# A convolution's backward pass: the input gradient's first three chunks with both outer leaves made from differences, the second gelu backward in channel halves, and a new order

## The chip, the cores and the metric

The kernel runs on one core of a Trainium2 chip. The metric is the device time of one execution in microseconds (us). In the listings PE is TensorE (PEld its weight loads), DVE is VectorE, ACT is ScalarE, POOL is GpSimd, and SP is the engine that issues most DMAs. "Weight load" and "matmul" are instructions; L1136 is line 1136 of the kernel.

## What is computed

A strided convolution along time (31 taps, stride 2, 256 channels in and out, two samples of 16000 steps, 7985 outputs), a group norm over time per channel, and a gelu; the outputs are the forward result and the gradients of x, w, gamma and beta.

```python
def _fwd_reference(x, w, gn_gamma, gn_beta):
    s = 2
    L = (T - K) // s + 1
    h = jnp.einsum('blc,cd->bld', x[:, 0:s * L:s, :], w[0])
    for i in range(1, K):
        h = h + jnp.einsum('blc,cd->bld', x[:, i:i + s * L:s, :], w[i])
    mu = jnp.einsum('bld->bd', h)[:, None, :] / L
    var = jnp.einsum('bld->bd', (h - mu) ** 2)[:, None, :] / L
    h = (h - mu) / jnp.sqrt(var + 1e-5)
    h = h * gn_gamma[None, None, :] + gn_beta[None, None, :]
    return _gelu(h)

def reference(x, w, gn_gamma, gn_beta, grad_out):
    _out, _vjp = jax.vjp(_f, x, w, gn_gamma, gn_beta)
    _grads = _vjp(grad_out)
    return (_out0, *[jnp.asarray(_g) for _g in _grads])
```

## The kernel before

**Stages.** The forward convolution of both samples (helpers named `f_`, matmuls at L506) runs first, with sample 0's gelu and gelu backward beside its second half. Then comes the input gradient (`input_grad`, matmuls at L1136): sample b = 0, chunks c = 0 to 3, then sample 1, chunks 0 to 3. The text numbers these t = 4b + c, 0 to 7. Last is the weight gradient (matmuls at L1351). Sample 1's gelu backward (`gelu_short`, eight units called by `gelu_batch`) runs beside the input gradient of sample 0; chunk 4 cannot begin before it has ended, since sample 1's gradient before the norm needs sums over the whole sample. Those sums are accumulated by ACT at L943, put together on DVE by `elem_finalize` (from the reduction at L978 on), and used by `e_load` and `e_comp` (L1015, L1017, L1033), which make the tile `ET` that a chunk starts from.

**A fast convolution of two levels.** The taps are split in a way that replaces four products of halves by three, first over branches (`br`: A, B, C), then over leaves (`lf`: A, B, C). A chunk is two halves (`pr`, 128 rows each) times three branches, so six units. A unit works in two PSUM tiles of 1024 fp32 columns. `g_three_b` and `g_three_ac` make the middle leaf B; its value is the seed for both outer leaves. Then the unit's outer leaves are made in the next unit's time, by the call `last(A)` and `last(C_)`:

- where (b, c, br) is in `GOC` ("both"), a third level of the same trick is used for the outer leaves as well. `g_outer` (4 matmuls) makes a product shared by two outputs, once with leaf C and once with leaf A. ACT copies it (`g_copy` into PSUM, `g_delta` into the tile `GSD`, L1165), DVE makes the seed with a subtraction (`g_seed`, L1199), and each outer leaf then takes 8 matmuls in `g_three_ac`, with differences that `third_two` makes on DVE. Such a unit has 36 matmuls. The results are evacuated by ACT (`keep`, L585), and DVE adds the middle branch for both leaves in one instruction of 2048 columns (L1213);
- elsewhere the seed is one copy by ACT (L585 inside PSUM), each outer leaf takes 16 matmuls in `g_leaf`, and DVE evacuates each of the two with the addition in it (L1217). Such a unit has 44 matmuls.

Before, branch B is always of the first kind, A and C from chunk 3 on. The weight sums that the first kind needs for A and C (`w2_outer`) are made after chunk 2.

**Gelu backward of sample 1.** One unit is one (c, e), 2048 columns, both channel halves (`dh`) side by side. ACT makes y and z from h (L916), DVE works on z (L920, L923), ACT makes two sigmoids (L926), DVE goes on (L920, L923), SP stores the result, ACT sums (L943, already by half). The tiles h and s come in rings of two, y and z in rings of one, grad_out in a ring of one.

**Staging.** After each chunk's first half `dl_turn` writes nine planes to DRAM for the weight gradient: for each, SP issues two transposes into a staging tile of the ring `DNO` (L319), and POOL two stores to `dld` (L314). The ring has four tiles. Since a plane (`GL`, `GS`, `ET`) is overwritten in the next chunk, its transposes must be over by then.

**Order.** Each engine works in program order, and its own queue of waits holds all that is behind. The program order is a table of operation numbers, `SEQUENCE`, made beforehand; `Plan.emit` issues operations in its order. Tiles have fixed addresses in one `arena`.

Of the kernel before, what the change touches and what calls it, by code (L numbers as in the profile page):

```python
# [1693 lines left out]
```

## Time and profile before

| | |
|---|---|
| runs | 1113.3, 1113.68, 1115.04 us |
| median | 1113.68 us |
| span of the profiled execution | 1111.2 us |

The span reaches from the first to the last instruction; what an execution takes beyond it lies around the program. The profiled execution's own time is not listed apart from its span; the median of the runs lies 2.5 us above that span. A group's row gives its line, engine, operation, shapes and count, then busy time in us and the mean of one in ns, then the engine's idle time just before it and what ended that.

### The profile page before, as it was taken

Reading aid. Unit: us, or ns where it says so; the run is one execution under the profiler, and the core shown is the slowest. Engines: PE = TensorE matmul, PEld = TensorE weight load, DVE = VectorE, ACT = ScalarE, POOL = GpSimd, SP = SyncE. Lnnn points to the kernel's source line nnn. Section 1 sums busy time; section 2 is a strip of 40 time slices with the busy share of each in tenths; the row PEclk is TensorE's granted clock in tenths of the full one; section 3 lists DMA queues with packets and bytes.
Section 4 is the critical chain, followed back from the end, with each engine's and each line's share of the span. In section 5 each row is a group of like instructions: output and inputs, shape, how many; then the busy total and the mean of one; then the engine's idle time right before and its main releaser. Section 6 shows DMA issues by size and latency. Waiting matters only on the chain.

```text
span 1111.2 us, 18967 instructions
## 1 busy us (share of the span) xinstructions
PE 1086.2 (98%) x7623; PEld 749.8 (67%) x7672; DVE 919.9 (83%) x900; ACT 578.9 (52%) x880; POOL 129.3 (12%) x233
## 2 busy tenths in 40 slices
PE   6999999999999989999999999999999999999998
PEld 4888899878787974444444444444587776678885
DVE  7987877889999999989897565644789699699995
ACT  1234434587988569899964566545413322111221
POOL 0000000000001003232332432251200000000000
PEclk9999999999999999999999999999999999999999
DMA  9979899876969789999999898577994959978888
GB/s 231 198 188 249 233 275 267 219 167 162 209 166 219 240 328 270 274 252 265 217 225 237 179 203 183 157 201 197 278 293 137 270 156 298 303 254 279 282 253 207
DMA packets 348806, 256.16 MB, mean 231 GB/s; under 512 B 234327, under 2 KB 315869, under 8 KB 343517
## 3 DMA queue, kind: packets, MB, share of 16 engines
q1 hardware_dynamic: 341613, 236.05, 81.8%
q0 software_dynamic: 7104, 18.89, 6.3%
q8 instruction: 60, 0.98, 0.4%
q14 instruction: 29, 0.24, 0.1%
HBM read 114.62 MB, written 84.45 MB: 179 GB/s over the span
## 4 chain that ended last, share of the span: by engine, by line
PE 89%; DVE 5%; issue 2%; DMA 1%; SPq 1%; ACT 1%; DVEq 0%
PE ps L1136 34%; PE ps L506 34%; PE ps L1351 21%; SPq L314 1%; DMA out_dram<-arena 1%; DVE arena L1437 1%; DVE ps L1461 1%; DMA arena<-in_w_dram 1%; DVE arena L1421 1%; DVE arena L1380 1%; DVE arena L1525 0%; DVE arena L581 0%; DVE arena L1417 0%; DVE arena L448 0%; DVE arena L1316 0%
## 5 line engine op out<-in xcount | busy, mean ns | idle before, releaser
L506 PE MATMUL ps<-arena 128*128 128x256 bf16 (+4 forms) x3464 | 396.6, 278 | 11.2 <-DMA arena<-in_x_dram 4.7
L1136 PE MATMUL ps<-arena 128*128 128x512 bf16 (+1 forms) x1787 | 388.1, 376 | 5.7 <-ACT ps L1165 3.6
L506 PEld LDWEIGHTS <-arena 128*128 128x128 bf16 x3464 | 338.2, 98 | 69.4 <-DMA arena<-in_x_dram 5.8
L1136 PEld LDWEIGHTS <-arena 128*128 128x128 bf16 x1824 | 178.5, 98 | 215.1 <-issue 2.9
L1351 PE MATMUL ps<-arena 128*128 128x256 bf16 (+1 forms) x2372 | 301.6, 289 | 3.4 <-DVE arena L1520 1.8
L1351 PEld LDWEIGHTS <-arena 128*128 128x128 bf16 x2384 | 233.2, 98 | 71.9 <-issue 2.3
L585 ACT ACTIVATE arena<-ps 128x1024 bf16<-128x1024 f32 (+1 forms) x121 | 122.1, 1022 | 213.0 <-PE ps L1351 77.3
L464 DVE TENSOR_TENSOR arena<-arena 128x2064 bf16<-128x2064 bf16 (+7 forms) x131 | 162.7, 1265 | 24.2 <-PE ps L506 23.0
L314 POOL DMA_DIRECT2D dld<-arena x144 | 104.6, 728 | 246.7 <-DMA arena<-arena 229.4
L1199 DVE TENSOR_TENSOR ps<-ps,arena 128x1024 f32<-128x1024 f32 x36 | 44.3, 1232 | 64.2 <-PE ps L1136 53.2
L1082 DVE TENSOR_TENSOR arena<-arena 128x1032 bf16<-128x1032 bf16 (+1 forms) x114 | 89.5, 813 | 9.5 <-POOL arena L1049 4.3
L551 ACT ACTIVATE ps<-ps 128x256 f32<-128x256 f32 x89 | 36.7, 412 | 85.6 <-PE ps L506 84.5
L1316 DVE TENSOR_TENSOR arena<-arena 128x4096 bf16<-128x4096 bf16 x30 | 68.3, 2287 | 0.5 <-DMA arena<-in_x_dram 0.3
L1165 ACT COPY ps<-ps 128x512 f32<-128x512 f32 x84 | 48.1, 575 | 33.7 <-PE ps L1136 30.0
L323 POOL MEMSET arena<- 128x104 bf16 (+11 forms) x52 | 12.0, 249 | 414.8 <-DVE arena L464 157.6
L923 DVE TENSOR_TENSOR arena<-arena 128x2048 bf16<-128x2048 bf16 (+1 forms) x48 | 57.5, 1197 | 3.0 <-ACT arena L926 1.3
L605 ACT ACTIVATE arena<-ps 128x512 bf16<-128x512 f32 (+1 forms) x64 | 37.0, 582 | 32.7 <-PE ps L506 28.2
L885 DVE TENSOR_TENSOR arena<-arena 128x2048 bf16<-128x2048 bf16 (+1 forms) x40 | 47.7, 1197 | 4.0 <-ACT arena L879 1.7
L1437 DVE TENSOR_TENSOR arena<-arena 128x2048 bf16<-128x2048 bf16 x40 | 48.5, 1220 | 2.4 <-PE ps L1351 2.4
L1461 DVE TENSOR_TENSOR ps<-ps,arena 128x1024 f32<-128x1024 f32 x24 | 29.1, 1227 | 19.5 <-PE ps L1351 19.5
L1453 ACT COPY ps<-ps 128x256 f32<-128x256 f32 x54 | 19.0, 360 | 47.8 <-PE ps L1351 46.7
L1525 DVE TENSOR_TENSOR arena<-arena 128x4608 bf16<-128x4608 bf16 x16 | 40.6, 2554 | 0.0
(92 smaller groups left out, 752.3 us busy)
## 6 DMA issues: line engine op xcount, KB each, us to landing
arena<-in_x_dram SPq DMA_DIRECT2D x36, 1024.0 KB
arena<-hd SPq DMA_DIRECT2D x40, 512.0 KB
dld<-arena POOLq DMA_DIRECT2D x144, 128.0 KB, 4.4
out_dram<-arena SPq DMA_DIRECT2D x14, 1024.0 KB
arena<-dld SPq DMA_DIRECT2D x18, 640.0 KB
arena<-dld SPq DMA_DIRECT2D x18, 576.0 KB
vl<-arena SPq DMA_DIRECT2D x36, 256.0 KB
arena<-vl SPq DMA_DIRECT2D x9, 1024.0 KB
```

The costliest lines, as they stand in the source:

```text
L314: lambda: e.dma_start(out=out, in_=in_), dma=np_ * ns / 16e3 * 1.03, ns=ns, tp=SH[pk], slack=slack)
L464: lambda: nc.vector.tensor_tensor(out=o, in0=a, in1=b, op=ALU.add))
L506: yield nc.tensor.matmul(ps[:, dh, cs], lhsT=wt, rhs=mv, start=s0, stop=False, skip_group_check=True)
L585: lambda: nc.scalar.activation(out=out, in_=ps, func=ACT.Copy, scale=scale))
L885: add("DVE", dve(nf), [o], [a, b_], lambda: V.tensor_tensor(out=o, in0=a, in1=b_, op=op))
L923: add("DVE", dve(nf), [o], [a, b_], lambda: V.tensor_tensor(out=o, in0=a, in1=b_, op=op))
L1082: lambda: nc.vector.tensor_tensor(out=o, in0=a, in1=b, op=ALU.subtract))
L1136: yield nc.tensor.matmul(ps[:, e, 0:wide], lhsT=lt, rhs=mv, start=s0, stop=False, skip_group_check=True)
L1165: add("ACT", act(512), [o], [i], lambda: nc.scalar.copy(out=o, in_=i))
L1316: add("DVE", dve(4096), [o], [a, b], lambda: nc.vector.tensor_tensor(out=o, in0=a, in1=b, op=ALU.add))
L1351: yield nc.tensor.matmul(ps[:, s, c0:c1], lhsT=lt, rhs=mv, start=s0, stop=False, skip_group_check=True)
L1437: add("DVE", dve(2048), [o], [u, v], lambda o=o, u=u, v=v: nc.vector.tensor_tensor(out=o, in0=u, in1=v, op=ALU.subtract))
```

## The change

- `GOC` now holds all branches of all chunks: in chunks 0 to 2, branches A and C become units of the first kind, 36 matmuls instead of 44. All weight sums of `w2_outer` are made ahead of the input gradient.
- `gelu_short` works on one channel half at a time: 16 half units instead of 8 units, with tiles of half the size in rings of the same counts; each half has its own load of h, its own store, and its own chain over ACT and DVE.
- Addresses move. The staging ring `DNO` has two tiles in chunks 0 to 3 (four before in chunks 0 to 2, four in chunk 3) and five after them. One of the two lies where the second `GSD` tile lies, so sample 0 uses one `GSD`, sample 1 two. `HO` (the input gradient's output tile) is one tile in all of sample 0, two in sample 1.
- `SEQUENCE` is new throughout, the forward and the weight gradient included. The matmuls of these two stages are the same in number.

```diff
@@ SEQUENCE
-7 10 4 1 11 8 5 9 2 13 3 6 12 20 14 15 36 30 38 39 29 35 32 40 33 31 24 34 37 23 41 42 50 48 47 45 21 51 44 49 46 43 22 53 59 54 26 52 64 28 60 83 84
...
+3511 3516 3503 3513 3517 3504 3505 3514 3518 3515
...
@@ tiles
-    HO = [sb(119232, 2, 4, 512), sb(GREG + 16704, 2, 4, 512)]
+    HO = [sb(119232, 2, 4, 512), sb(GREG + 20544, 2, 4, 512)]
...
-    DNO = {True: [sb(GREG + 28928 + 2048 * i, 2, 2, D) for i in range(4)], False: [sb(GREG + o, 2, 2, D) for o in (0, 2048, 25088, 27136)]}
+    DNO = {True: [sb(o, 2, 2, D) for o in (208960, 113088)], False: [sb(o, 2, 2, D) for o in (208960, *(GREG + 28736 + 2048 * i for i in range(4)))]}
...
@@ gelu_batch
-        tiles = [ring_of(k, 2, 4, HM) for k in rings]
+        tiles = [ring_of(k, *((2, 4, HM) if b == 0 else (4, HM))) for k in rings]
...
+                    for dh in range(2):
+                        gelu_short(b, c, e, dh, [r[(2 * n + dh) % len(r)] for r in tiles], go[:, dh])
...
@@ gelu_short
-    def gelu_short(b, c, e, tiles, go, oo):
+    def gelu_short(b, c, e, dh, tiles, go):
...
-        load(full[0].rearrange("p d k f -> p d (k f)"), hv, 524288, 2048, "ACT")
+        load(full[0].rearrange("p k f -> p (k f)"), hv, 262144, 2048, "ACT")
...
-        nf = 8 * wd
+        nf = 4 * wd
...
@@ dl_turn
-                ds = DNO[4 * b + c < 3]
+                ds = DNO[4 * b + c < 4]
...
-    gsc = [0]
+    gsc, bnow = [0], [0]
 
     def g_delta(pt):
-        gsc[0] += 1
-        g_copy(GSD[gsc[0] % 2], pt[:, 0])
+        gsc[0] = 1 - gsc[0] if bnow[0] else 0
+        g_copy(GSD[gsc[0]], pt[:, 0])
...
-        ho = HO[pr if both else 0]
+        ho = HO[pr if b else 0]
...
-    GOC = {(b, c, br) for b in range(NB) for c in range(NCK) for br in ORDER if 4 * b + c >= 3 or br == B_}
+    GOC = {(b, c, br) for b in range(NB) for c in range(NCK) for br in ORDER if (b, c, br) not in ()}
...
@@ the calls
-        if br == B_:
-            for lf in (C_, A):
-                w2_outer(lf, (B_,))
+        for lf in (C_, A):
+            w2_outer(lf, (MIR[br],))
...
-        if (b, c, pr, br) == (0, 2, 1, A):
-            for lf in (C_, A):
-                w2_outer(lf, (A, C_))
```

The first place is ACT in the middle of chunks 0 to 2. L943 is a sum of gelu, L916 its first two functions, L926 its sigmoids; L1165 is a copy of a shared product, L585 a seed (ps<-ps) or an evacuation (arena<-ps). Before:

```order
L943 ACTIVATE arena,esum_113<-arena 128x1024 x6
L1165 COPY ps<-ps 128x512
L916 ACTIVATE arena<-arena,stats 128x1024 x4
L585 ACTIVATE ps<-ps 128x1024
L585 ACTIVATE arena<-ps 128x1024
L926 ACTIVATE arena<-arena 128x2048 x2
L1165 COPY ps<-ps 128x512
L585 ACTIVATE arena<-ps 128x1024
```

The same engine in the changed kernel, where these lines are L951, L925, L935, L1173 and L591:

```order
L1173 COPY ps<-ps 128x512
L925 ACTIVATE arena<-arena,stats 128x1024
L591 ACTIVATE arena<-ps 128x2x512
L1173 COPY ps<-ps 128x512 x2
L1173 COPY arena<-ps 128x512
L951 ACTIVATE arena,esum_113<-arena 128x1024
L925 ACTIVATE arena<-arena,stats 128x1024
L951 ACTIVATE arena,esum_113<-arena 128x1024
L1173 COPY ps<-ps 128x512
L935 ACTIVATE arena<-arena 128x1024 x2
L591 ACTIVATE arena<-ps 128x2x512
```

Runs of one kind are gone: each half unit's few rows alternate with copies and evacuations of the convolution, of which there are more, and no row copies a seed any more.

The second place is DVE at the end of sample 1's gelu backward: the reduction of its sums (L978) and what follows to the scaling of chunk 4's tile (L1017, L1015, L1033). L1217 and L1199 belong to units of chunks 2 and 3, L452 and L1234 are weight sums. Before:

```order
L978 TENSOR_REDUCE small<-esum_113 128x4
L1082 TENSOR_TENSOR arena<-arena 128x2x516
L1217 TENSOR_TENSOR arena<-ps,arena 128x2x512
L980 TENSOR_TENSOR small<-stats,small 128x2
L1199 TENSOR_TENSOR ps<-ps,arena 128x1024
L1234 TENSOR_TENSOR arena<-arena 128x2048
L981 TENSOR_TENSOR small<-small 128x2
L452 TENSOR_TENSOR arena<-arena 128x2048
L982 TENSOR_TENSOR small<-stats 128x2
L983 TENSOR_TENSOR small<-stats,small 128x2
```

In the changed kernel (L932 the last gelu operations, L986 the reduction, L1023 and L1041 the scaling and the spreading into chunk 4's tile):

```order
L932 TENSOR_TENSOR arena<-arena 128x4x232 x3
L986 TENSOR_REDUCE small<-esum_113 128x4
L988 TENSOR_TENSOR small<-stats,small 128x2
L989 TENSOR_TENSOR small<-small 128x2
L990 TENSOR_TENSOR small<-stats 128x2
L991 TENSOR_TENSOR small<-stats,small 128x2
L992 SCALAR_TENSOR_TENSOR stats<-small 128x2
L993 SCALAR_TENSOR_TENSOR small<-small,stats 128x2
L994 TENSOR_TENSOR small<-stats 128x2
L995 SCALAR_TENSOR_TENSOR stats<-small 128x2
L1023 TENSOR_SCALAR arena<-arena,stats 128x2048
L1041 TENSOR_TENSOR arena<-arena 128x2x3x256
```

Work of the convolution that stood between these rows has moved ahead of them: on PE, 220 matmuls followed the reduction up to chunk 4's first before, and 44 do now.

More of the change, by code (lines that the diff above doesn't have):

```diff
@@ L350, in conv_stem_kernel @@
     GS = sb(190336, 2, 2, 2, 2, EM)
-    GL = {B_: sb(198656, 2, 2, 2, EM), A: sb(202816, 2, 2, 2, EM), C_: sb(102656, 2, 2, 2, EM)}
-    GU = {B_: sb(206976, 2, 2, EM), A: sb(106816, 2, 2, EM), C_: sb(108928, 2, 2, EM)}
+    GL = {B_: sb(198592, 2, 2, 2, EM), A: sb(202720, 2, 2, 2, EM), C_: sb(102656, 2, 2, 2, EM)}
+    GU = {B_: sb(206848, 2, 2, EM), A: sb(106816, 2, 2, EM), C_: sb(108928, 2, 2, EM)}
     GREG = 127424
-    HO = [sb(119232, 2, 4, 512), sb(GREG + 16704, 2, 4, 512)]
+    HO = [sb(119232, 2, 4, 512), sb(GREG + 20544, 2, 4, 512)]
     GSB = sb(115136, 2, 2, 512)
     GSD = [sb(o, 512, dt=FP32) for o in (111040, 113088)]
-    W2DO = {B_: sb(173696, 2, 2, 512), C_: sb(GREG + 29184, 2, 2, 512), A: sb(GREG + 33280, 2, 2, 512)}
-    GU2 = {br: sb(o, 2, 2, 2, 260) for br, o in zip(ORDER, (94336, 94336 + 4160, GREG + 12288))}
-    W2DC = {B_: sb(177792, 2, 2, 512), C_: sb(GREG + 4096, 2, 2, 512), A: sb(GREG + 8192, 2, 2, 512)}
-    DNO = {True: [sb(GREG + 28928 + 2048 * i, 2, 2, D) for i in range(4)], False: [sb(GREG + o, 2, 2, D) for o in (0, 2048, 25088, 27136)]}
-    assert GREG + 37952 <= REG
-    DG, DGT = sb(209664, P), sb(209920, P)
+    W2DO = {B_: sb(173696, 2, 2, 512), C_: sb(GREG, 2, 2, 512), A: sb(GREG + 4096, 2, 2, 512)}
+    W2DC = {B_: sb(177792, 2, 2, 512), C_: sb(GREG + 8192, 2, 2, 512), A: sb(GREG + 12288, 2, 2, 512)}
+    GU2 = {br: sb(o, 2, 2, 2, 260) for br, o in zip(ORDER, (94336, 94336 + 4160, GREG + 16384))}
+    DNO = {True: [sb(o, 2, 2, D) for o in (208960, 113088)], False: [sb(o, 2, 2, D) for o in (208960, *(GREG + 28736 + 2048 * i for i in range(4)))]}
+    assert GREG + 37184 <= 164608
+    DG, DGT = sb(164608, P), sb(164864, P)
     ident = DGT
@@ L850, in gelu_batch @@
                 oo = oos[n % len(oos)]
-                (gelu_unit if b == 0 else gelu_short)(b, c, e, [r[n % len(r)] for r in tiles],
-                                                      gt.rearrange("p k d f -> p d k f")[:, :, :, off:off + HM], oo)
+                go = gt.rearrange("p k d f -> p d k f")[:, :, :, off:off + HM]
+                if b == 0:
+                    gelu_unit(b, c, e, [r[n % len(r)] for r in tiles], go, oo)
+                else:
+                    for dh in range(2):
+                        gelu_short(b, c, e, dh, [r[(2 * n + dh) % len(r)] for r in tiles], go[:, dh])
                 n += 1
@@ L908, in gelu_short @@
         full = tiles
-        h, y, s, z, go = (t[:, :, :, 0:wd] for t in (*tiles, go))
-        hv, dv = (d[b][c][:].rearrange("p (d e f) -> p d e f", d=2, e=2)[:, :, e] for d in (h_d, dy_d))
-        load(full[0].rearrange("p d k f -> p d (k f)"), hv, 524288, 2048, "ACT")
-        for dh in range(2):
-            for o, k, fn in ((y, 7, ACT.Identity), (z, 9, ACT.Square)):
-                sc, bi = st(b, k, dh), st(b, k + 1, dh)
-                add("ACT", act(4 * wd, 0.18), [o[:, dh]], [h[:, dh], sc, bi],
-                    lambda o=o, dh=dh, sc=sc, bi=bi, fn=fn: SC.activation(out=o[:, dh], in_=h[:, dh], func=fn, bias=bi, scale=sc))
-        nf = 8 * wd
+        h, y, s, z, go = (t[:, :, 0:wd] for t in (*tiles, go))
+        hv, dv = (d[b][c][:].rearrange("p (d e f) -> p d e f", d=2, e=2)[:, dh, e] for d in (h_d, dy_d))
+        load(full[0].rearrange("p k f -> p (k f)"), hv, 262144, 2048, "ACT")
+        for o, k, fn in ((y, 7, ACT.Identity), (z, 9, ACT.Square)):
+            sc, bi = st(b, k, dh), st(b, k + 1, dh)
+            add("ACT", act(4 * wd, 0.18), [o], [h, sc, bi],
+                lambda o=o, sc=sc, bi=bi, fn=fn: SC.activation(out=o, in_=h, func=fn, bias=bi, scale=sc))
+        nf = 4 * wd
         def plus(o, k):
@@ L935, in gelu_short @@
         tt(s, y, go, ALU.mult)
-        load(dv, full[2].rearrange("p d k f -> p d (k f)"), 524288, 2048, "POOL")
+        load(dv, full[2].rearrange("p k f -> p (k f)"), 262144, 2048, "POOL")
         tt(y, s, h, ALU.mult)
@@ L939, in gelu_short @@
         for i, t, jk in ((0, s, h), (1, y, y)):
-            for dh in range(2):
-                a0, v, j = esum[b][:, dh, i, u:u + 1], t[:, dh], jk[:, dh]
-                add("ACT", act(4 * wd, 0.19), [j, a0], [v],
-                    lambda j=j, v=v, a0=a0: SC.activation(out=j, in_=v, func=ACT.Copy, accum_out=a0))
+            a0 = esum[b][:, dh, i, u:u + 1]
+            add("ACT", act(nf, 0.19), [jk, a0], [t],
+                lambda jk=jk, t=t, a0=a0: SC.activation(out=jk, in_=t, func=ACT.Copy, accum_out=a0))
     def out0_store(b, c, e, oo):
@@ L1195, in g_seed @@
             return
-        t = GSD[gsc[0] % 2]
+        t = GSD[gsc[0]]
         i = bass.AP(tensor=t.tensor, offset=t.offset, ap=[list(t.ap[0]), [0, 2], [1, 512]])
@@ L1244, in input_grad @@
                 plan.part = c
+                bnow[0] = b
                 first, second, third, third_two, planes, leaf = g_sums(t)
@@ L1634, in conv_stem_kernel @@
     e_load(0, 0)
-    ge = gelu_batch(1, GREG, *RINGS[1], *PACE[1])
+    ge = gelu_batch(1, GREG + 20544, *RINGS[1], *PACE[1])
     for b, c, pr, br, leaf in input_grad():
```

215 rows, old and new, of the table SEQUENCE are left out of this document.

## The prediction

> **What bounds the kernel now.** First the page's totals and the chain that ended last:
>
> ```profile
> span 1111.2 us, 18967 instructions
> PE 1086.2 (98%) x7623; PEld 749.8 (67%) x7672; DVE 919.9 (83%) x900; ACT 578.9 (52%) x880; POOL 129.3 (12%) x233
> ...
> PE 89%; DVE 5%; issue 2%; DMA 1%; SPq 1%; ACT 1%; DVEq 0%
> ```
>
> TensorE is busy for 98% of the span and carries 89% of the chain, so a matmul less looks like time saved. An average over stages may deceive, so next the busy time by stage. The cuts: 408, first matmul of the input gradient; 621, first of its chunk 4 (where sample 1 begins); 801, first of the weight gradient. The columns are stretch, length, then busy time (count) of PE, PEld, DVE, ACT, POOL, then clock, DMA share, GB/s.
>
> ```profile
> 0.00:408.00 408.00, 396.63 (x3464) 338.16 (x3464) 355.62 (x375) 230.94 (x430) 8.40 (x28) 1.00 0.90 221
> 408.00:463.00 55.00, 51.79 (x237) 23.68 (x243) 53.54 (x73) 51.28 (x64) 12.39 (x19) 1.00 1.04 278
> 463.00:516.00 53.00, 52.08 (x243) 24.06 (x246) 48.86 (x52) 47.69 (x56) 18.15 (x31) 1.00 1.05 260
> 516.00:567.00 51.00, 50.74 (x237) 23.54 (x241) 45.43 (x51) 44.59 (x57) 17.53 (x34) 1.00 0.94 223
> 567.00:621.00 54.00, 53.74 (x249) 24.68 (x252) 43.39 (x61) 29.25 (x42) 17.33 (x27) 1.00 0.96 237
> 621.00:801.00 180.00, 179.10 (x827) 82.45 (x842) 98.67 (x104) 101.98 (x133) 52.82 (x91) 1.00 0.80 196
> 801.00:1112.00 311.00, 302.12 (x2376) 233.25 (x2385) 274.38 (x189) 73.11 (x107) 2.69 (x4) 1.00 0.83 249
> ```
>
> The change lies in the stage from 408 to 621, where sample 1's gelu backward runs beside chunks 0 to 3. Over its 213 us PE is busy 51.79 + 52.08 + 50.74 + 53.74 = 208.4, DVE 191.2, ACT 172.8: PE sets the pace, with DVE 17 us behind. In the first 55 us DVE is busy for 97%. From 621 on DVE and ACT are busy little over half the time. The waits of PE between 408 and 801 are small:
>
> ```profile
> PE ps L1136 <- ACT ps L1165: 3.6, 4, 1.1
> PE ps L1136 <- DVE arena L1082: 0.2, 1, 0.2
> ```
>
> **The change, part by part.** The durations come from the groups of the same stage, 408 to 621, kept apart by shape (count | busy us, mean ns | idle before):
>
> ```profile
> L923 DVE TENSOR_TENSOR arena<-arena 128x2048 bf16<-128x2048 bf16 x36 | 44.0, 1223 | 1.8 <-ACT arena L916 0.4 <-ACT arena L926 0.3
> L1082 DVE TENSOR_TENSOR arena<-arena 128x1032 bf16<-128x1032 bf16 x51 | 34.3, 689 | 0.2
> L1217 DVE TENSOR_TENSOR arena<-ps,arena 128x1024 bf16<-128x1024 f32 x24 | 28.8, 1219 | 6.5 <-PE ps L1136 5.4 <-issue 1.0
> L943 ACT ACTIVATE arena<-arena 128x1024 bf16<-128x1024 bf16 x24 | 25.1, 1047 | 2.1 <-DVE arena L923 2.0
> L585 ACT ACTIVATE arena<-ps 128x1024 bf16<-128x1024 f32 x24 | 24.2, 1019 | 12.4 <-PE ps L1136 12.4
> L926 ACT ACTIVATE arena<-arena 128x2048 bf16<-128x2048 bf16 x12 | 22.9, 1909 | 0.9 <-DVE arena L923 0.8
> L926 ACT ACTIVATE arena<-arena 128x1856 bf16<-128x1856 bf16 x4 | 7.0, 1746 | 0.0
> L1165 ACT COPY ps<-ps 128x512 f32<-128x512 f32 x39 | 22.2, 573 | 10.9 <-PE ps L1136 10.1 <-DVE arena L1217 0.4
> L1199 DVE TENSOR_TENSOR ps<-ps,arena 128x1024 f32<-128x1024 f32 x12 | 14.8, 1230 | 5.8 <-PE ps L1136 4.1 <-ACT arena L1165 1.5
> L1082 DVE TENSOR_TENSOR arena<-arena 128x2064 bf16<-128x2064 bf16 x12 | 14.6, 1228 | 1.3 <-PE ps L1136 1.2
> L923 DVE TENSOR_TENSOR arena<-arena 128x1856 bf16<-128x1856 bf16 x12 | 13.4, 1120 | 1.2 <-ACT arena L926 1.0
> L585 ACT ACTIVATE ps<-ps 128x1024 f32<-128x1024 f32 x12 | 12.1, 1006 | 4.9 <-PE ps L1136 3.3 <-remote 1.6
> L920 DVE TENSOR_SCALAR arena<-arena 128x2048 bf16<-128x2048 bf16 x12 | 8.3, 689 | 0.2
> L1213 DVE TENSOR_TENSOR arena<-arena 128x2048 bf16<-128x2048 bf16 x3 | 3.7, 1226 | 4.1 <-ACT arena L585 4.1
> ```
>
> *PE.* Twelve units (chunks 0 to 2, two halves, branches A and C) go from 44 matmuls to 36: 96 fewer, 84 of them 512 wide and 12 of 256. The stage has 982 weight loads in 208.4 us, and nearly all its matmuls are 512 wide, so one takes about 0.215 us. The saving is 84 × 0.215 + 12 × 0.108 = 19.4 us, and PE's need falls from 208.4 to 189.
>
> Here a rule speaks against the size of this term. The Trainium skill, "TensorE: Matmul & The Clock Gate", section "Back-to-back issue gap", gives about 131 ns for a matmul of 512 columns in a stream of weight load and matmul pairs; by it the estimate of the saving would be 96 × 0.131 = 12.6 us at most. The trace has such pairs and disagrees (0.215 us), so I keep 19.4.
>
> *ACT.* Each of the twelve units gains two 512-wide copies (L1165: 24 × 0.573 = +13.8) and two evacuations (L585 into the arena: 24 × 1.019 = +24.5) and loses the copying seed (12 × 1.006 = −12.1). The 16 sigmoids become 32 halves. No row shows a half; L943 has its size, and 24 × 1.047 + 8 × 0.97 − 29.9 (the whole ones, 22.9 + 7.0) gives +3; an exact halving gives 0, and no halving at all +30, for which the 1.047 leaves no room. The sum is +29. Neighbours overlap:
>
> ```profile
> 418.01 4.63 ACT L916 ACTIVATE arena<-arena,stats 128x1024 bf16<-128x1024 bf16 x4
> ```
>
> Four here take 4.63 us, where four single ones of 1.23 would take 4.9, so 0.1 is hidden per neighbour. For 52 more instructions I take off 5: +24, and ACT's need is 197.
>
> *DVE.* Gains twelve seeds (12 × 1.230 = +14.8), twelve wide adds (L1213: 12 × 1.226 = +14.7) and six sums `third_two` (2064 wide: 6 × 1.228 = +7.4); loses 24 evacuations (24 × 1.219 = −29.3). Gelu's 48 two-tensor operations become 96 halves: 72 × 0.689 + 24 × 0.63 (0.689 scaled to 928 wide) − 44.0 − 13.4 = +7.3. Its 16 additions of a constant become 32: between 0 (an exact halving) and +11 (a half as long as the 0.689 of a whole); I take +5, as two-tensor halves keep 0.08 above half and these have more fixed time in them. Overlap takes off 0.08 for each of 70 more, −6. That is +14; about 6 us of the stage's sums and weight sums now stand ahead of 408, beside the forward's last matmuls. DVE's need is about 199.
>
> *DMA and queues.* SP issues 16 more loads and stores of half size, about 0.6 us each (the row of 418.91 below) in a queue with idle time: 9 us, all hidden at best, all lost if gelu waits for each; I take the first, since the next half's load may run ahead by a tile. The staging ring of the gradient planes goes from four tiles to two in chunks 0 to 3; that is priced among the rivals. Single `GSD` in sample 0: the next delta waits for the seed before it, a unit (7.7 us) earlier, so nothing. `HO` 0 alone in chunk 3: as chunks 0 to 2 have it now, nothing.
>
> *The rest.* Forward and weight gradient keep their matmuls, in a new order. PE stood still there for 11.4 and 8.9 us, of which a first load, some short releases and the tail make most; I take 0, and 3 us either way.
>
> *The sum.* The needs of the stage are now PE 189, ACT 197, DVE 199. PE no longer sets its length. Two engines almost full, with a chain that goes between them four times per gelu half, reach what the first 55 us show for DVE, 97%: 199 / 0.97 = 205 instead of 213. At 100% it is 199 (−14); at the 93% that DVE shows from 408 to 567 (147.8 of 159) it is 214 (+1). The end is pinned: chunk 4 needs sample 1's statistics, and these need its last gelu half. Before, these came 50 us ahead of chunk 4:
>
> ```profile
> 568.86 0.96 ACT L943 ACTIVATE arena<-arena 128x928 bf16<-128x928 bf16 x1
> 569.72 0.19 ACT L943 ACTIVATION_READ_ACCUMULATOR arena<-arena 128x1 f32 x1
> 570.90 0.18 DVE L978 TENSOR_REDUCE small<-esum 128x4 f32<-128x32 f32 x1
> ```
>
> That cover goes. In the new order, as the second place shown with the change tells, statistics, scaling and chunk 4's sums follow each other on DVE, so the lateness falls on PE at once: **11 us of the 19.4 are given back there**. The forecast is 8 us off the span, 1103; the median of the runs, 1113.68, lies 2.5 us over this span, so it is **1106**.
>
> **The rivals.** *PE stays the bound* (the two engines keep up, the halves fit exactly): −19.4 plus 2 of waits, 1096. Against it: both other needs exceed 189. 13%.
>
> *Nothing moves*: 93% of DVE, or a staging tile at today's turnaround, as below. 1113. 17%.
>
> *Slower: the staging ring of two.* A tile is filled by two transposes on SP, emptied by two stores on POOL, and free when both have landed. One round, from SP, POOL and the issue table of 408 to 616:
>
> ```profile
> 416.23 2.63 SPq L319 DMA_TRANSPOSE arena<-arena  x2
> 418.91 0.57 SPq L314 DMA_DIRECT2D arena<-dyd  x1
> 419.53 4.28 SPq L319 DMA_TRANSPOSE arena<-in_grad_out_dram  x1
> ...
> 423.22 1.55 POOL L314 DMA_DIRECT2D dld<-arena  x2 [22.96 <-DMA arena<-arena]
> dld<-arena POOLq DMA_DIRECT2D x72, 128.0 KB, 4.1
> ```
>
> From 416.23 to about 424.0 + 4.1 = 428.1 it is 11.9 us. Four tiles allow a plane every 3 us; two, every 6, and the 36 planes of chunks 0 to 3 take 214 us. Each plane's transposes must be through before the next chunk overwrites it, and a transpose that waits holds SP's queue, with gelu's loads behind it. The decisive point is a round of 205 / 18 = 11.4 us: below it the ring is hidden, and each 0.5 us above costs 9. For it: the DMA share is already 0.94 to 1.05. Against: 416.23 is a busy moment (a transpose of grad_out follows), and a ring that is waited for has shorter queues. At 12.5 us a round, 225 us: +12, 1126. 20%.
>
> *A cold array.* If PE's lateness falls in one gap at chunk 4, the matmuls behind it may start slow. In the rows above the clock is 1.00 throughout, but the longest wait is 1.1 us. The Trainium skill, same page, section "HAM oscillation — how this bites in real kernels", has gaps over about 3.4 us drop the clock to half; by it 3.4 us of matmuls would take twice as long. As a mechanism here: 16 matmuls at 0.215 more, 1106 + 3.4 = 1109. 3%.
>
> **How the numbers follow.** The forecast (1106) has 47%, 1113 has 17%, 1126 20%, 1096 13%, 1109 3%. What is under 0.2%, 2.2 us, a measurement of this kernel can hardly tell from no change. Faster: 47 less 3 that end near zero, plus 13 and 3, so 0.60; same 0.18; slower 0.22. The range runs from PE's bound, 1095, to half way into the slow case, 1121; about one in ten lies outside at each end.
>
> **What would show it.** Between the stage's first matmul and chunk 4's: PE's matmul time near 189 us, DVE and ACT busy over 95%, PE waiting 10 to 16 us in all, mostly just before chunk 4. From chunk 4 to the end no difference over 3 us. If PE's waits are small, the first rival holds. If SP's transposes wait for stores (dld), with DVE and ACT idle, the ring holds; if the forward or the weight gradient changes by more than 3 us, the new order did more than I gave it.

## The result, and the profile after

The changed kernel takes **1176.6 us** (median of 4 runs, 1173.73 to 1182.07) against 1113.72 us (4 runs, 1113.3 to 1115.04): a ratio of 1.057, with a 95% interval of 1.054 to 1.060. It is slower by 63 us, where 8 us faster was forecast, and lies far outside the range of 1095 to 1121. The profiled execution took 1173.73 us, 1.8 us more than its span.

First the totals and the chain that ended last, as shown of before:

```profile
span 1171.9 us, 18989 instructions
PE 1085.8 (93%) x7529; PEld 743.0 (63%) x7576; DVE 939.0 (80%) x970; ACT 604.1 (52%) x932; POOL 126.0 (11%) x233
...
PE 22%; DMA 17%; DVE 11%; SPq 6%; issue 5%; ACT 5%; POOL 1%; POOLq 0%; DVEq 0%; ACTq 0%
```

TensorE carried 89% of the chain before and carries 22% now. Transfers, DVE, ACT and SP's own queue took its place, so TensorE waits. The stages show where. The cuts are first weight loads: 435.7 of the input gradient, 484.0, 540.9 and 594.4 of its chunks 1 to 3, 658.2 of chunk 4, 852.9 of the weight gradient. A chunk is counted from the first load of its middle leaf, and the 621 of the prediction is this mark too; the very first load of chunk 4, for a shared product, stands 4.1 us ahead of it (2.6 before). Columns as before: stretch, length, busy time (count) of PE, PEld, DVE, ACT, POOL, clock, DMA share, GB/s.

```profile
0.00:435.70 435.70, 403.21 (x3464) 340.36 (x3465) 363.50 (x382) 234.55 (x427) 8.10 (x28) 0.98 0.83 208
435.70:484.00 48.30, 44.83 (x202) 19.69 (x205) 44.60 (x70) 46.43 (x66) 11.36 (x18) 1.00 0.99 263
484.00:540.90 56.90, 50.06 (x218) 21.88 (x221) 49.19 (x70) 49.01 (x67) 16.20 (x28) 0.97 0.88 225
540.90:594.40 53.50, 46.62 (x209) 20.64 (x212) 48.36 (x68) 49.12 (x66) 14.41 (x30) 1.00 0.87 217
594.40:658.20 63.80, 53.53 (x233) 23.41 (x237) 49.27 (x76) 48.99 (x69) 14.93 (x26) 0.97 0.71 182
658.20:852.90 194.70, 184.81 (x841) 84.18 (x857) 108.34 (x118) 102.48 (x135) 55.13 (x96) 0.99 0.77 198
852.90:1172.00 319.10, 302.77 (x2374) 232.79 (x2384) 275.78 (x190) 73.53 (x106) 5.85 (x9) 1.00 0.82 245
```

| stage | before, us | after, us | difference |
|---|---|---|---|
| forward | 408.0 | 435.7 | +27.7 |
| chunks 0 to 3 | 213.7 | 222.5 | +8.8 |
| chunks 4 to 7 | 179.6 | 194.7 | +15.1 |
| weight gradient and tail | 309.9 | 319.0 | +9.1 |

Every stage is longer, those too whose operations did not change. The mark of chunk 4 does not divide the work alike: 984 weight loads of the input gradient stood ahead of it, now 872 do, 112 fewer where the edit takes out 96. So 16 loads, 3.4 us of TensorE, have passed from chunks 0 to 3 into chunks 4 to 7. In the forward TensorE has the same 3464 matmuls, yet it stands idle for 435.7 − 403.2 = 32.5 us (11.4 before) and is busy 6.6 us longer. In the input gradient its idle time is 417.2 − 379.9 = 37.3 us; before it was 393 − 387.4 = 5.6. In the changed stage the work came out near the forecast: ACT 193.6 us (forecast 197), DVE 191.4 (199), TensorE 195.0 (189). No engine fills it: 195.0 of 222.5 is 88%.

Now the waits (waiting line, what it waited for: us in all, times, longest), TensorE's in the forward:

```profile
PE ps L512 <- DVE arena L470: 9.1, 7, 2.9
PE ps L512 <- DVE arena L454: 8.5, 1, 8.5
PE ps L512 <- DMA arena<-in_x_dram: 5.7, 2, 4.6
PE ps L512 <- ACT ps L557: 5.7, 5, 2.2
```

Before, only the first load had its like there; the next longest row was `PE ps L506 <- DVE arena L448: 1.7, 2, 1.1`. From 436 to 658 the longest row of TensorE, then of SP, and SP's like row of before (408 to 622), are:

```profile
PE ps L1144 <- ACT ps L1173: 16.2, 14, 3.3
```

```profile
SPq L325 <- DMA dld<-arena: 51.2, 23, 7.1
```

```profile
SPq L319 <- DMA dld<-arena: 4.4, 3, 2.3
```

SP's row is that of its transposes, which wait for stores (`dld`) to free a staging tile: 51.2 us, and 4.4 before. The chain that ended last, in order of time, shows a stretch of this (start, us, what; dots stand for pieces left out):

```profile
604.57 1.27 SPq L325
...
606.58 1.23 SPq L325
...
607.86 3.06 DMA arena<-arena
...
611.44 0.72 POOL dld L320
612.16 4.68 DMA dld<-arena
...
616.97 1.25 SPq L325
...
618.27 2.52 DMA arena<-arena
...
620.86 1.85 issue
622.72 0.43 POOL dld L320
...
623.45 5.36 DMA dld<-arena
...
628.86 1.19 SPq L325
```

Transposes on SP, their landing, stores on POOL, their landing, and 0.1 us after it the next transpose. One tile's round here goes from 606.58 to 616.84, 10.3 us, its next from 616.97 to 628.81, 11.8. Through all of chunks 0 to 3 each tile was occupied in this way for 96 and 97% of the time between its first transpose (441.4, 430.5) and its last landing (677.0, 662.6): 226.8 us in 18 rounds for the one, 12.6 a round. A few long rounds lift this mean; the medians of the two tiles are 11.2 and 11.5 us. The longest, 34.1 us from 630.2 on, comes from a place in the new order: its transposes had been issued by 634, but in the program its second store stands on POOL behind the stores of two later planes and was issued at 658.5.

### The profile page after: what moved, and what is told of

Read it like the earlier page. It is cut to its first block, busy times and chain, and to the rows that moved or that the text cites. A ratio compares the mean times of both kernels' runs of the same rounds, so it can differ in the third digit from the quotient of the medians.

```text
span 1171.9 us, 18989 instructions
## 1 busy us (share of the span) xinstructions
PE 1085.8 (93%) x7529; PEld 743.0 (63%) x7576; DVE 939.0 (80%) x970; ACT 604.1 (52%) x932; POOL 126.0 (11%) x233
## 4 chain that ended last, share of the span: by engine, by line
PE 22%; DMA 17%; DVE 11%; SPq 6%; issue 5%; ACT 5%; POOL 1%; POOLq 0%; DVEq 0%; ACTq 0%
PE ps L1360 13%; PE ps L1144 9%; DMA dld<-arena 6%; DMA arena<-arena 4%; SPq L325 4%; SPq L320 2%; DMA arena<-hd 1%; POOL dld L320 1%; ACT arena L591 1%; DVE arena L1534 1%; DVE arena L1325 1%; DMA arena<-dyd 1%; PE ps L512 1%; DMA dyd<-arena 1%; DVE arena L1090 1%
## 5 line engine op out<-in xcount | busy, mean ns | idle before, releaser
L512 PE MATMUL ps<-arena 128*128 128x256 bf16 (+4 forms) x3464 | 403.4, 280 | 32.5 <-DVE arena L470 9.1
L1144 PE MATMUL ps<-arena 128*128 128x512 bf16 (+1 forms) x1693 | 380.1, 380 | 37.3 <-ACT ps L1173 19.8
L1144 PEld LDWEIGHTS <-arena 128*128 128x128 bf16 x1728 | 169.8, 98 | 247.3 <-issue 51.2
L591 ACT ACTIVATE arena<-ps 128x1024 bf16<-128x1024 f32 (+1 forms) x145 | 144.8, 1018 | 229.5 <-PE ps L1360 75.7
L470 DVE TENSOR_TENSOR arena<-arena 128x2064 bf16<-128x2064 bf16 (+8 forms) x131 | 163.1, 1264 | 25.8 <-DMA arena<-in_x_dram 20.7
L320 POOL DMA_DIRECT2D dld<-arena x144 | 104.8, 729 | 304.2 <-DMA arena<-arena 244.4
L1207 DVE TENSOR_TENSOR ps<-ps,arena 128x1024 f32<-128x1024 f32 x48 | 59.0, 1229 | 56.7 <-PE ps L1144 51.9
L1090 DVE TENSOR_TENSOR arena<-arena 128x1032 bf16<-128x1032 bf16 (+1 forms) x120 | 96.9, 835 | 6.0 <-DMA arena<-arena 2.0
L1325 DVE TENSOR_TENSOR arena<-arena 128x4096 bf16<-128x4096 bf16 x30 | 68.6, 2288 | 11.6 <-DMA arena<-in_x_dram 11.2
L932 DVE TENSOR_TENSOR arena<-arena 128x1024 bf16<-128x1024 bf16 (+1 forms) x96 | 64.9, 676 | 14.0 <-DMA arena<-in_grad_out_dram 6.0
L1173 ACT COPY ps<-ps 128x512 f32<-128x512 f32 x96 | 55.3, 577 | 37.2 <-PE ps L1144 36.5
L329 POOL MEMSET arena<- 128x78 bf16 (+11 forms) x52 | 10.6, 227 | 420.7 <-DVE arena L470 300.8
L1221 DVE TENSOR_TENSOR arena<-arena 128x2048 bf16<-128x2048 bf16 x32 | 39.1, 1221 | 19.2 <-ACT arena L591 18.8
L895 DVE TENSOR_TENSOR arena<-arena 128x2048 bf16<-128x2048 bf16 (+1 forms) x40 | 47.7, 1199 | 7.1 <-ACT arena L887 3.6
L1446 DVE TENSOR_TENSOR arena<-arena 128x2048 bf16<-128x2048 bf16 x40 | 48.0, 1218 | 1.2 <-PE ps L1360 1.1
L972 ACT ACTIVATE arena<-arena,stats 128x1024 bf16<-128x1024 bf16 x16 | 19.4, 1237 | 53.3 <-DMA arena<-hd 51.5
```

The costliest lines, as they stand in the source:

```text
L320: lambda: e.dma_start(out=out, in_=in_), dma=np_ * ns / 16e3 * 1.03, ns=ns, tp=SH[pk], slack=slack)
L470: lambda: nc.vector.tensor_tensor(out=o, in0=a, in1=b, op=ALU.add))
L512: yield nc.tensor.matmul(ps[:, dh, cs], lhsT=wt, rhs=mv, start=s0, stop=False, skip_group_check=True)
L591: lambda: nc.scalar.activation(out=out, in_=ps, func=ACT.Copy, scale=scale))
L932: add("DVE", dve(nf), [o], [a, b_], lambda: V.tensor_tensor(out=o, in0=a, in1=b_, op=op))
L1090: lambda: nc.vector.tensor_tensor(out=o, in0=a, in1=b, op=ALU.subtract))
```

## Which order, which stage

The lengths of stages in this section come from each run's own profile; "chunks" are those of the input gradient, W is the weight gradient from its first weight load to its last. Times of before, after, b_re, halves, a_only and full_re are medians of four runs, the others of a single one. Runs of the changed kernel differ by up to 8 us (the four above), so smaller differences of single runs' totals are not read.

| run | time, us | forward | chunks 0-3 | chunks 4-7 | W |
|---|---|---|---|---|---|
| before | 1113.7 | 408.0 | 213.7 | 179.6 | 304.1 |
| after | 1176.6 | 435.7 | 222.5 | 194.7 | 311.9 |
| start | 1175.7 | 429.5 | 222.0 | 199.2 | 315.2 |
| f_old | 1176.3 | 415.7 | 238.8 | 198.1 | 314.4 |
| fw_old | 1165.8 | 415.4 | 236.9 | 201.2 | 304.1 |
| b_fnew | 1148.8 | 438.0 | 215.6 | 179.6 | 307.6 |
| b_ring2 | 1158.5 | 407.9 | 258.7 | 179.8 | 304.1 |
| a_still | 1171.3 | 439.3 | 216.1 | 193.9 | 313.3 |
| fw_still | 1153.5 | 415.3 | 231.0 | 194.1 | 304.9 |
| act_short | 1176.9 | 435.4 | 221.6 | 197.7 | 313.0 |
| a_goc | 1221.8 | 436.8 | 269.9 | 197.3 | 310.4 |
| b_re | 1153.5 | 421.0 | 211.6 | 186.4 | 323.0 |
| halves | 1167.8 | 426.1 | 220.8 | 189.2 | 320.9 |
| a_only | 1174.8 | 418.3 | 227.5 | 190.0 | 326.5 |
| full_re | 1163.5 | 419.6 | 219.7 | 191.5 | 323.1 |
| sp_g | 1178.6 | 436.9 | 227.5 | 194.0 | 310.7 |
| fw_sp | 1171.8 | 420.4 | 242.0 | 197.4 | 304.4 |
| b_fsp | 1146.2 | 440.5 | 214.6 | 179.6 | 303.8 |
| hoist | 1183.2 | 430.4 | 227.6 | 197.2 | 318.3 |
| b_fhoist | 1142.8 | 431.9 | 219.1 | 179.6 | 304.2 |

**The order alone.** Four kernels differ from before or after only in `SEQUENCE`. Operations 0 to 1260 are the forward's, the same in both kernels.

```diff
@@ start: SEQUENCE of after
-60 56 85 66 87 57 86 82 88
+60 66 82 56 85 87 57 86 88
@@ f_old: after, the places of operations 0 to 1260 filled in the order of before
-10 5 1 2 11 4 8 9 6 20
+7 10 4 1 11 8 5 9 2 13
...
@@ fw_old: f_old, and the weight gradient's 601 operations likewise
...
@@ b_fnew: before, the places of operations 0 to 1260 filled in the order of after
-7 10 4 1 11 8 5 9 2 13
+10 5 1 2 11 4 8 9 6 20
...
```

> The changed kernel with two operations moved in the order: the weight differences second and third of the first tap group on DVE (L470, 128x8x260) stand ahead of the three transposing loads of x that follow them in time, as before; nothing else differs. Theory ORDER (the new program order holds engines on transfers they do not need): DVE's wait of 9.6 us at 22 us and PE's of 8.5 us on DVE L454 go, the first matmul of the input gradient comes 8 to 10 us earlier than 435.7, and the time is 1166 to 1169 us against 1176.6. Theory WORK (the loss comes from the edit's own work and its ring; waits early in the forward are made up later): 1174 to 1178 us.

> The changed kernel with the forward's 1261 operations in the relative order they had before; input gradient and weight gradient keep the new order. Theory ORDER: the input gradient begins at 408 to 411 us instead of 435.7, all later stages keep their lengths, 1147 to 1151 us. Theory WORK: the forward is slow for another reason (addresses, contention by what is issued beside it) and the start stays over 425; 1166 us or more.

> As the run before it (forward in its old order), and the weight gradient's 601 operations in their old relative order as well. Theory ORDER: the weight gradient takes 305 us instead of 312.7, so 1139 to 1143 us. Theory WORK: the weight gradient stays at 312 to 313 us, and the time is that of the run with the forward alone put back, within 2 us.

> The kernel before with the new relative order of the forward's 1261 operations; nothing of the edit is in it, the input gradient and the weight gradient keep their old order. Theory ORDER: the forward takes 434 to 438 us, and the time is 1138 to 1144 us. Theory WORK: the forward stays near 408 and the time within 4 us of 1113.7.

b_fnew is the plain case: without any of the edit, the forward's new order makes the forward 30.0 us longer and the kernel 34.7 (beside 1114.07 on the same chip). Of the 30.0, TensorE is busy 5.9 us longer (402.5 against 396.6) and idle 24.1 longer. TensorE's waits in it have the changed kernel's signature:

```profile
PE ps L513 <- DVE arena L455: 9.1, 1, 9.1
PE ps L513 <- DVE arena L471: 8.7, 7, 3.1
PE ps L513 <- ACT ps L558: 6.0, 5, 2.3
```

The row of 9.1 us, the 8.5 above, is one place in the first 30 us. DVE's timeline of the changed kernel shows it (start, us, operation, idle time ahead of it):

```profile
12.23 0.68 DVE L454 TENSOR_TENSOR arena<-arena 128x1024 bf16<-128x1024 bf16 x1
22.47 2.39 DVE L470 TENSOR_TENSOR arena<-arena 128x2080 bf16<-128x2080 bf16 x2 [9.55 <-DMA arena<-in_x_dram]
24.78 5.88 DVE L454 TENSOR_TENSOR arena<-arena 128x2048 bf16<-128x2048 bf16 x5
```

Two sums of x (L470, operations 66 and 82) waited for a transposing load of x. In the kernel's own table they do not depend on it; it stood ahead of them in the program. The weight differences (L454) that TensorE wanted stood behind them on DVE. In start this wait is gone and the forward is 6.2 us shorter. The time is not: the later stages take that much longer. f_old wins 20 us in the forward and loses 16 in chunks 0 to 3; chunk 4 begins at 654.5 instead of 658.2. So in the changed kernel something else holds chunk 4. The forward of f_old is still 7.7 us over before's; one wait of 5.1 us, `PE ps L519 <- DVE ps L594`, is most of that, and its cause is open. fw_old then takes 10.5 us off, and W is 304.1, exactly before's: the 8 us there are the order's. Theory ORDER (the new order of unchanged operations costs the time) holds for the weight gradient and for 20 of the forward's 27.7 us, and fails for the claim that the losses add up.

**The staging ring.**

```diff
@@ b_ring2: before, order kept but for what two tiles force
-                ds = DNO[4 * b + c < 3]
+                ds = DNO[4 * b + c < 3][:2 if 4 * b + c < 4 else 4]
@@ a_still (after) and fw_still (fw_old): dl_turn, what is stored
-P=P), o[:, j], 131072, 512,
+P=P), (sb(73728, 2, 2, D) if 4 * b + c < 4 else o)[:, j], 131072, 512,
@@ act_short: gelu_short of after, the sums
-SC.activation(out=jk, in_=t, func=ACT.Copy, accum_out=a0))
+SC.activation(out=jk[:, :, 0:16], in_=t[:, :, 0:16], func=ACT.Copy, accum_out=a0))
```

> The kernel before, with two of its four staging tiles used in chunks 0 to 3; its order is kept, but for the stores and transposes that two tiles put behind one another. Nothing else of the edit is in it. Theory RING (two staging tiles hold SP, and through SP's queue everything that is loaded, in chunks 0 to 4): the stage of chunks 0 to 3 grows from 213.7 to 220 to 230 us, SP waits 40 us or more for stores, 1121 to 1135 us. Theory FULL (DVE and ACT, filled by the edit, set the stage): stage and time stay within 3 us of 213.7 and 1114.

> The changed kernel with the order unchanged, in which the stores of chunks 0 to 3 read a tile that stays still instead of the staging tile, so that a staging tile is free once its transposes have landed; transfers are the same in number and size. It leaves out the right values of those planes for the weight gradient. Theory RING: chunks 0 to 3 take 203 to 212 us instead of 222.5, chunks 4 to 7 180 to 185 instead of 194.7, SP waits for no store there, 1145 to 1157 us against 1176.6. Theory FULL: chunks 0 to 3 stay at 220 to 224, and the time at 1172 or more.

> Both at once: forward and weight gradient in their old order (that run took 1165.8 us, with 415.4, 236.9, 201.2 and 304.1 us for forward, chunks 0 to 3, chunks 4 to 7, weight gradient), and the stores of chunks 0 to 3 from a tile that stays still, as in the run before; the same values are left out. Theory RING with ORDER: the two losses add up, chunks 0 to 3 take 205 to 220, chunks 4 to 7 180 to 186, forward and weight gradient stay: 1106 to 1127 us. Theory FULL: chunks 0 to 3 stay over 230, 1160 us or more.

> The changed kernel with ACT's 32 sums of sample 1's gelu backward (L951, 1.05 us each) taken over 64 columns of the 928 or 1024: some 24 us less of ACT's work in chunks 0 to 3, about what the edit added there, and nothing else changed. It leaves out most of the terms of those sums. Theory FULL (ACT at 87% of the stage keeps TensorE's copies waiting behind gelu): chunks 0 to 3 take 203 to 213 us instead of 222.5, in all 1157 to 1168 us. Theory TRANSFER (staging tiles and loads that land late hold the stage, and ACT only waits in turn): 218 us or more, 1171 us or more.

b_ring2: two tiles alone, in an order made for four, cost 44.4 us (beside 1114.07 on the same chip), all in chunks 0 to 3, which are 45.0 longer. SP's waits there:

```profile
SPq L326 <- DMA dld<-arena: 70.8, 22, 6.8
```

act_short takes 24 us of work from ACT, as much as the edit was to add, and the stage stays: 221.6 against 222.5. The work taken away became waits. The stage's busy times, SP's longest wait and ACT's longest:

```profile
435.40:656.90 221.50, 195.47 (x874) 85.63 (x872) 189.60 (x280) 169.66 (x265) 55.70 (x100) 0.98 0.83 218
```

```profile
SPq L325 <- DMA dld<-arena: 60.6, 21, 7.4
```

```profile
ACT arena L925 <- DMA arena<-hd: 13.7, 7, 4.9
```

ACT fell from 193.6 to 169.7, SP waits 60.6 us instead of 51.2, and gelu's loads of h come late, because they stand in SP's queue behind the transposes. So ACT's fullness does not set the stage. Freeing the ring does less than it should, though: in a_still SP waits for no store from 439 to 655, and the stage takes 216.1, not the 203 to 212 expected. With the ring free the stage is 6 us shorter (start and act_short, which keep the ring and TensorE's order, have 222.0 and 221.6), and a second limit holds it there:

```profile
439.30:655.40 216.10, 195.74 (x875) 85.77 (x874) 190.29 (x280) 193.00 (x265) 52.01 (x93) 0.98 0.89 225
```

TensorE 91%, ACT 89%, DVE 88% of 216.1. Chunks 4 to 7 were expected at 180 to 185 us and took 193.9, 0.8 less than with the ring. fw_still gives as much for the stage: 231.0 against fw_old's 236.9; chunks 4 to 7 are 7 us shorter too, and 12 us are off the time. But it was expected at 1106 to 1127 and took 1153.5: with forward and weight gradient in their old order and the ring free, 40 of the 63 us are left, 7.3 in the forward, 17.3 in chunks 0 to 3 and 14.5 in chunks 4 to 7. What makes them is not shown. In every kernel made from after, the input gradient has an order other than before's, and the addresses are the moved ones; no run puts the old ones back. Theory RING (the staging ring of two holds chunks 0 to 3) is right about the first limit and wrong about its size; theory FULL (ACT and DVE, nearly full, hold them) is wrong for the ring as it is, and what holds at 216 with the ring free (ACT's work was not cut there) stays open.

**The edit in parts, and orders searched anew.** a_goc makes A and C of chunks 0 to 2 as before, in the rest of after's order. The other four have an order searched by moving single operations; an order was valued by letting each engine run its operations in that order with their durations, a transfer landing 3 to 5 us after its issue. full_re has the whole edit, halves only gelu by halves, a_only this and branch A from differences; the two use the space left for more staging tiles. b_re, the control, is before in an order found likewise.

```diff
@@ a_goc: GOC of after
-for br in ORDER if (b, c, br) not in ()}
+for br in ORDER if 4 * b + c >= 3 or br == B_}
@@ a_only (in halves, EARLY holds B_ alone, with two more tiles)
+    EARLY = {0: (B_, A), 1: (B_, A), 2: (B_, A)}
-for br in ORDER if (b, c, br) not in ()}
+for br in ORDER if 4 * b + c >= 3 or br in EARLY[4 * b + c]}
-(208960, 113088)]
+(208960, 113088, GREG + 4096, GREG + 6144, GREG + 12288, GREG + 14336)]
-                ds = DNO[4 * b + c < 4]
+                ds = DNO[4 * b + c < 3]
```

> The changed kernel with the outer leaves of A and C in chunks 0 to 2 made as before (44 matmuls a unit, one copy for a seed, evacuations on DVE); gelu halves, staging ring of two, addresses and the order of all that is left are those of the changed kernel. PE's need in chunks 0 to 3 is 208 us again, ACT's 24 and DVE's some 7 us less. Theory FULL: with room on DVE and ACT the stage is PE's again, 211 to 216 us instead of 222.5. Theory RING: the stage stays at 220 to 228 us and the time at 1174 to 1184 us.

> The changed kernel's operations, tiles and staging ring of two, unchanged, in another order: one searched so that no engine stands behind a transfer when a transfer is given some 3 to 5 us from issue to landing. Theory SLACK (the loss comes from an order that leaves transfers no time to land, so that engines and SP stand in their queues; the edit itself fits): forward 402 to 412 us, chunks 0 to 3 203 to 212, chunks 4 to 7 182 to 188, weight gradient 303 to 308, in all 1098 to 1118 us. Theory WORK (two staging tiles and fuller DVE and ACT cost what they cost in any order): chunks 0 to 3 stay at 220 us or more, 1122 us or more.

> The control: the kernel before, its order searched in the same way from its own order. Theory SLACK: little to win, as its order leaves transfers time already: 1098 to 1112 us, chunks 0 to 3 205 to 213. If this one lies below the full edit searched anew, the edit pays nothing even with a good order; if it lies 3 us or more above, the edit pays.

> The gelu halves alone: outer leaves of A and C in chunks 0 to 2 as before, eight staging tiles in chunks 0 to 2 in the space that this leaves, order searched in the same way. DVE gets some 12 us more work, PE keeps its 208. Theory SLACK: the stage of chunks 0 to 3 stays PE's, 209 to 214 us, in all 1106 to 1118 us. Theory WORK: the halves alone cost 6 us or more in that stage (219 or more).

> The gelu halves, and the outer leaves from differences for branch A alone in chunks 0 to 2 (48 matmuls fewer, 10 us of PE), with six staging tiles in chunks 0 to 2 and the order searched in the same way. Theory SLACK: DVE sets the stage, 203 to 211 us, in all 1100 to 1114 us. Theory WORK: 216 us or more in that stage.

a_goc took 270 us for the stage, outside both theories: its 72 replaced operations were fitted into an order made for others. It tells nothing on the edit.

All four miss the totals that theory SLACK gave. Those of theory WORK (the edit costs in any order) come: full_re is over 1122 us, and its stage of 219.7 is just short of the 220 it asked for; halves and a_only have 220.8 and 227.5 where it asked for 219 and 216. But the control misses as well: before's own operations in a searched order take 1153.5 us (ratio 1.0354, interval 1.0330 to 1.0377), 40 us more than in the order they had. So before's order holds something that this way of valuing orders does not see, and theory SLACK, that time for transfers is enough, falls. Compared with one another, as orders made in the same way, they say less: full_re 1163.5 (ratio 1.0454, 1.0420 to 1.0487) is 10.0 us slower than b_re, halves 14.2, a_only 21.2. a_only stands between the other two in what it does and is 7 us slower than the slower of them, so orders found in this way scatter by as much or more, and what each part of the edit is worth is not read from them. All that carry gelu by halves are slower than the one without; none shows a gain. The stage of chunks 0 to 3 of b_re and of full_re:

```profile
421.00:632.50 211.50, 205.45 (x942) 93.76 (x960) 190.12 (x230) 167.90 (x208) 60.34 (x105) 1.00 0.98 250
```

```profile
419.60:639.30 219.70, 196.63 (x852) 85.77 (x869) 196.80 (x284) 193.86 (x260) 57.76 (x102) 0.97 0.91 225
```

Without the edit TensorE fills 97% of its stage; with it DVE fills 90%, TensorE 89% and ACT 88%, with SP's waits for stores down to 26.5 us.

**One engine's order, and single places.** sp_g (on after) and fw_sp (on fw_old) move only SP's operations in the input gradient, b_fsp those of the forward in b_fnew, with the two sums of start. hoist and b_fhoist move only instructions of ACT and DVE that TensorE waited for.

```diff
@@ sp_g, fw_sp, b_fsp: SP's operations sorted by
-    the time of issue
+    max(time at which what it needs was ready, time of issue - 8 us; b_fsp: 6 us)
@@ hoist (54 instructions), b_fhoist (13): an instruction on ACT or DVE that ended a wait of TensorE
-    behind the instruction it stood behind
+    at max(time at which what it needs was ready, its start - 5 us)
```

> The changed kernel with SP's operations of the input gradient in another order: each at the time at which, by the profile of the changed kernel, what it needs was ready (at most 8 us earlier than it was issued), so that a transpose that waits for its staging tile stands behind loads that could go. PE, ACT and DVE keep their orders. Theory SPQ (transposes that wait for staging tiles hold the loads behind them in SP's queue): SP's waits for stores fall under 60 us between 436 and 853, chunks 4 to 7 take 181 to 188 us instead of 194.7, chunks 0 to 3 212 to 219 instead of 222.5, in all 1155 to 1168 us. Theory ENG (the order of PE, ACT and DVE is what costs): chunks 4 to 7 stay at 191 or more, and the time within 5 us of 1176.6.

> The same edit of SP's order on the kernel with forward and weight gradient in their old order (1165.8 us; 415.4, 236.9, 201.2, 304.1). Theory SPQ: chunks 0 to 3 215 to 228, chunks 4 to 7 182 to 190, in all 1135 to 1152 us. Theory ENG: 1158 us or more.

> The kernel before with the forward's new order (1148.8 us, forward 438.0), in which SP's operations of the forward stand by the time they could go (at most 6 us earlier than they were issued), and second and third of the first tap group ahead of the transposing loads of x as in the run named start. Theory SPQ: the forward takes 412 to 426 us, in all 1122 to 1137 us. Theory ENG: only the 6 us of the run named start are won, forward 430 to 434, 1140 to 1146 us.

> The changed kernel with 54 instructions moved ahead on ACT (32) and DVE (22): those that ended a wait of TensorE of over 0.3 us in its profile while they stood behind another instruction of their engine; each is put where what it needs was ready, at most 5 us earlier. PE and SP keep their orders. Theory PLACE (TensorE's waits are the order's: an instruction it needs stands a place or two too late, and the staging and loads only shift them): of the 75 us of waits that the profile shows between matmuls, 20 to 35 go, 1140 to 1158 us. Theory FULL (ACT and DVE are full in their stages, so what is overtaken comes late in its turn): the time stays within 8 us of 1176.6.

> The same on the kernel before with the forward's new order (1148.8 us, forward 438.0): 13 instructions of the forward moved ahead on ACT and DVE. DVE and ACT are far from full there. Theory PLACE: the forward takes 418 to 430 us, in all 1128 to 1141 us. Theory FULL makes no claim for the forward; if the waits come back elsewhere there, 1145 us or more, the cause is not the place of single instructions.

None of them shortens the input gradient, though in sp_g SP's waits for stores between 436 and its end fell from 103.2 to 64.8 us: theories SPQ (SP's order) and PLACE (single instructions in the wrong place) fall there. In hoist the row `PE ps L1151 <- ACT ps L1180` (after's L1173) fell to 11.1 us, and the wait for DVE's seeds rose from 3.9 to 8.4: what was overtaken came late in its turn. In the forward, b_fhoist won 6 of the 30 us, b_fsp nothing; in both the one long wait of TensorE in the first 30 us stays (8.4 and 9.2 us). So what is left of the forward's loss in b_fhoist, 24 us, is this wait, 5 us of longer busy time, and some 10 us more than before in waits of 0.3 to 3 us (16.7 against 6.4) that single moves do not mend. That the order as a whole makes them is shown by b_fnew; which property of it does is open.

## Why the prediction was wrong

- **"Forward and weight gradient keep their matmuls, in a new order … I take 0, and 3 us either way."** This step failed most: the forward took 27.7 us more, the weight gradient 7.8, together 35.5 of the 61 us by which the spans differ. The runs show that the order alone can do this (b_fnew, +30.0 in a kernel without the edit), and that in the changed kernel it does most of it (20 of the 27.7 go in f_old, all 7.8 in fw_old); in the total only the 10.5 us of fw_old come off. The matmuls were the right thing to count for work, and the wrong one for time: an order that had kept TensorE busy for 97% was replaced, and its worth, 40 us against a searched one (b_re), was priced at nothing. Only rows of before were used, and they can't show what a new order waits for; the bound should have been wide, above all upwards.
- **The staging ring, "20%".** This rival's mechanism held in the changed stage. It was priced as a round of 12.5 us with a stage of 225; the trace has a mean of 12.6 and 222.5. That they agree so well is in part luck: the median round is 11.2 and 11.5, at the decisive 11.4, and long rounds like the one of 34.1 us, which a store's place in the order made, lift the mean over it. The step that failed is the reason against it, "a ring that is waited for has shorter queues": in this stage a store lands 4.4 us after its issue (median), 4.2 before. What the rival did not hold is the rest: with the ring free the stage is 216, not 205.
- **"… reach what the first 55 us show for DVE, 97%: 199 / 0.97 = 205 instead of 213."** The needs were near (ACT 197 forecast, 193.6 measured; DVE 199 and 191.4). The fill was not: no run of the edit has DVE or ACT over 90% of the stage. The 97% came from one stretch of 55 us, in which ACT was at 93% and TensorE at 94%; no run of the edit kept that up over a stage. At 90%, the need of 193.6 gives 215, near a_still's 216.1; whether the fill of these engines is what holds a_still there was not tested.
- **"From chunk 4 to the end no difference over 3 us."** Chunks 4 to 7 took 15.1 us more, 3.4 of them by where the mark falls. The last transposes of chunk 3 landed at 669.8, 11.6 us behind the mark of chunk 4; before, at 612.4, 9.3 us ahead of it. This is not shown to be the cause, which stays open: without waits for stores in chunks 0 to 3, a_still still has 193.9 there, and fw_still 194.1 (201.2 with them). The term "11 of the 19.4 are given back there" saw lateness at this place, but of gelu's sums and bounded by TensorE's saving.
- **The saving, 19.4 us of TensorE,** was right as work: the input gradient has 1728 weight loads against 1824, and the spacing is 0.2155 us. It bought nothing, as TensorE was no longer the bound.
- **The cold array, "3%",** took part. The forecast had one gap at chunk 4; there were several, below. One stretch at half clock costs half of its 3.4 us, 1.7, where the forecast took 3.4.

The text named both signs that came: a change of over 3 us in forward or weight gradient "did more than I gave it", and SP's transposes waiting for `dld`. Its range had no case in which the order of unchanged work was worse.

## What to carry to other kernels

In a kernel with every engine in program order, an order is a part of the kernel like its tiles: a change that brings a new one for all stages has to be priced as two changes, and the new order's share has no upper bound in a profile of the old. Where a staging ring is cut, compare one round (issue, landing, store, landing) with the time between uses, and take the round at its busy value: being waited for did not make this one faster. A fill seen in one stretch of 55 us is not one to divide a whole stage's need by.

## What the runs showed of the hardware

TensorE's clock fell to half after idle stretches. Five stretches of the changed kernel, columns as above:

```profile
480.00:485.50 5.50, 5.45 (x28) 2.55 (x27) 4.45 (x7) 4.12 (x6) 1.07 (x3) 1.00 1.26 242
485.60:489.20 3.60, 0.49 (x3) 0.10 (x1) 1.74 (x4) 1.63 (x2) 0.32 (x1) 1.00 1.18 191
489.20:490.40 1.20, 1.06 (x5) 0.49 (x5) 1.20 (x3) 1.17 (x3) 0.77 (x2) 1.00 0.80 205
490.40:493.80 3.40, 3.40 (x10) 1.26 (x9) 3.27 (x5) 2.76 (x4) 0.68 (x1) 0.54 1.16 278
493.80:500.00 6.20, 6.13 (x29) 2.74 (x28) 4.44 (x8) 4.88 (x6) 1.44 (x2) 0.98 0.74 206
```

TensorE stood still for 3.3 us, up to 489.3; the clock held for 1.3 us of new work, then was at half for 3.4 us (0.54 in that row), in which the weight loads came every 0.43 us instead of 0.2155. In the input gradient 23 spacings are of this kind (0.41 to 0.45 us), 4.9 us more in all than at the usual spacing; none was before. Between the first 30 us and the tail the trace has four such falls, with idle stretches of 2.9, 3.3, 2.3 and 2.7 us that end at 215.0, 489.3, 654.1 and 702.0. One of 3.2 us, ending at 676.3, brought none. The Trainium skill, "TensorE: Matmul & The Clock Gate", section "HAM oscillation — how this bites in real kernels", has idle gaps over about 3.4 us bring the half clock; in this trace shorter ones did, and no run shows what decides. In the forward's first 30 us, with the wait of 8.5 us in them, the clock was 0.83 (1.00 before).

Unexpected too was that landing did not get slower: the median of the staging stores from issue to landing is 4.3 us, 4.4 before (4.4 and 4.2 in the changed stage alone). What changed is who stood and waited for it.
